# Attention and a squared-ReLU layer on one core: paired transposing DMAs, stores and squares moved to ScalarE, a split last store, and a new planned order

## The chip, the cores and the metric

One core of a Trainium2 chip runs the whole program. Its engines work side by side, each through its own list of instructions in order: TensorE (PE, matrix products into PSUM; PEld is its loading of weights), VectorE (DVE), ScalarE (ACT), GpSimd (POOL) and SyncE (SP). SP, ACT and POOL can issue DMA transfers. An engine waits on semaphores that other engines or landed transfers raise. The metric is the device time of one execution in microseconds (us).

## What is computed

```python
def _attn_ref(q, k, v):                    # (8, 8, 576, 64) each
    B, H, S, D = q.shape
    window = 32
    scores = 1.0 / np.sqrt(D) * np.matmul(q, k.transpose(0, 1, 3, 2))
    pos = np.arange(S)
    mask = np.abs(pos[:, None] - pos[None, :]) <= window
    scores = np.where(mask, scores, -1000000000.0)
    scores = scores - np.max(scores, axis=-1, keepdims=True)
    attn = np.exp(scores)
    attn = attn / (np.sum(attn, axis=-1, keepdims=True) + 1e-09)
    return np.matmul(attn, v).astype(np.float32)

def _moe_ref(x, w_in, w_out):              # (4608, 512), (512, 2048), (2048, 512)
    r = np.maximum(x @ w_in, 0.0)
    return ((r * r) @ w_out).astype(np.float32)

x = attn_out.transpose(0, 2, 1, 3).reshape(B * S, H * D)   # between the two
```

Inputs and the output are float32; the kernel computes its products in bfloat16.

## The kernel before

**Tiles.** The 8 batches of 576 tokens are 4608 tokens. Attention runs in 72 steps of 64 tokens (9 a batch, all 8 heads in one step): `scores` (L468) makes the products of queries with 128 keys (`sc`, line L478), ScalarE the exp (L483), VectorE the mask (L490); `av` (L493) makes the product with the values (`avp`, L505), the reciprocal of the sums (L517) and the scaling into `xr` (L519). `xturn` (L524) turns the step's result so that features lie on partitions, into the ring `xt` of 32 steps: for the first NPE = 26 steps by TensorE (`trp`, L537) and a ScalarE copy (L542), for the other 46 by a transposing DMA on SP (L529), one for each step.

The second half works on 9 tiles of 512 tokens. `mm1` (L547) multiplies `xt` with W1 (`w_in`) into one of two PSUM banks `ht` (products at L53 or, in the 128-token units of the first tile, L51). ScalarE takes the relu (L565), VectorE the square into `gt` (L569). There are 16 such units a tile, numbered k = 0 to 143 over the kernel. `mm2` (L573) multiplies `gt` with W2 (`w_out`) into `outp`, in four segments for each block of 128 tokens; after the fourth, ScalarE copies the block to SBUF (`oe`, L587) and SP stores it (L589). There are 36 blocks. `tile` (L592) records one tile's `mm1` units with the `mm2` segments of the tile before between them.

**Loads.** GpSimd issues all loads from HBM, since they convert to bfloat16. `FIRST` (L37) lists the first 39 in order: pieces of 128 tokens of q, k and v of batches 0 and 1 (the last piece of q and k is 64 tokens, `"e"` are the two ends of v), W1 in the chunks of `WCH` (`"a"`, L423) and W2 in quarters (`"b"`, L430). Batches 0 and 1 of q and k are turned by TensorE (`fine_turn`, L354: products at L364, then a VectorE copy for k, L373, and two ScalarE copies for q, L378). For batches 2 to 7, q and k are loaded raw (`load_qk`, L388), turned in 32x32 blocks by VectorE (`turn`, L438, eight instructions for each of q and k), and moved to their places by small transfers inside SBUF on SP (`spread`, L452, 16 a batch, from `kst` and `qst` to `kt` and `qz`). `copy_v` (L415) makes a copy of v that is shifted by half a tile.

**Order.** Nothing is ordered by hand. Each operation is recorded by `Prog.rec` with an engine, what it reads and writes, a key and an expected duration `dur`; a DMA has also `move` (packets, ns of each). `Prog.schedule` (L103) then runs a list scheduler when the program is built: at each engine, of the operations that its own times hold ready, the one with the lowest key goes next. The list for each engine is fixed by this, and on the chip an engine waits at an operation whose inputs are late although others behind it could run. A transfer is booked as landed 1700 ns after its last packet (`it[3].end = now + 1700` in `serve`, L139); the rings of POOL, SP and ACT take turns. In idle time of TensorE early in the program the planner sets products on a tile of zeros (`zz`), written to `outp`.

The constants at the top set the keys: `LEAD` of the attention steps, `FK`, `FQ` of the first turns, `TOFF`, `TOFF2`, `TST` and `TREL` (a gate) of the VectorE turns, `KQ` and `KVL` of the loads, `VK0`, `VK1`, `VK` of the copies of v, `KM`, `MD`, `TM` of the two products. `UNITS` (L32) is the order of the 16 units of the first tile: (first token, tokens, first of the 16 feature blocks), where feature blocks 4i to 4i + 3 read the i-th quarter of W1.

## Time and profile before

| | |
|---|---|
| median of 3 runs | 317.48 us (316.34, 317.48, 318.16) |
| the profiled execution | 320.36 us |
| its span, first to last instruction | 318.7 us |
| PE busy, products | 303.1 us in 4065 |
| PEld | 205.5 us |
| VectorE | 211.0 us |
| ScalarE | 165.1 us |
| GpSimd | 89.0 us |
| mean granted TensorE clock | 0.988 |
| DMA moved | 38.52 MB in 99291 packets |
| packets of POOL's queue, of SP's | 73136, 26112 |

How to read it: busy times are unions of an engine's instructions and say nothing of whether the work was wanted. Products are pipelined and their ends are modelled, so consecutive products overlap in the rows. The chain of waits goes back from the last instruction, at each step to what released it. In rows of a timeline the first number is the start in us from the span's start, the second the length, and a bracket gives the idle time before and what ended it; a q behind an engine's name is its list of DMA issues. Rows of DMA issues give the count, KB of each and the median us from issue to landing.

### The profile page before, as it was taken

To read this page: it belongs to the slowest core of one execution; us is meant where nothing else is said; L and a number is where in the kernel's file an instruction comes from. 1 tells how busy PE (TensorE), PEld (TensorE's weight loads), DVE (VectorE), ACT (ScalarE), POOL (GpSimd) and SP (SyncE) were. 2 spreads that over 40 slices of the span, in tenths; PEclk is the share of its full clock that TensorE was granted. 3 is DMA by queue.
4 is the path that set the end of the run, shared out by engine and by line. 5 is a ranking of instruction groups with operands and counts; after the bars stand their busy time and mean duration, and the time that the engine had idled before them with its cause. 6 is when DMAs were issued, how large, how long until landed. Compare 5 with 4: busy or idle time off the path is not lost.

```text
span 318.7 us, 9690 instructions
## 1 busy us (share of the span) xinstructions
PE 303.1 (95%) x4065; PEld 205.5 (64%) x4065; DVE 211.0 (66%) x529; ACT 165.1 (52%) x303; POOL 89.0 (28%) x128
## 2 busy tenths in 40 slices
PE   6798999998999999979989999999999999999995
PEld 2466887877977776757546666665665666556552
DVE  7475686958798888868848888898744444323300
ACT  2387767545835662446435645643654555435511
POOL 8999992432142324401504211100000000000000
PEclk9799999999999999999979999999999999999999
DMA  9999999999969948993999596635411211210021
GB/s 58 145 186 200 174 189 187 201 229 237 117 105 183 172 49 129 190 215 48 137 176 161 54 161 102 138 79 110 118 50 51 68 43 43 59 69 33 2 100 67
DMA packets 99291, 38.52 MB, mean 121 GB/s; under 512 B 72624, under 2 KB 93616, under 8 KB 99248
## 3 DMA queue, kind: packets, MB, share of 16 engines
q0 software_dynamic: 73136, 18.36, 60.2%
q1 hardware_dynamic: 26112, 19.54, 22.0%
q8 instruction: 32, 0.52, 0.7%
q14 instruction: 11, 0.09, 0.1%
HBM read 36.70 MB, written 9.44 MB: 145 GB/s over the span
## 4 chain that ended last, share of the span: by engine, by line
PE 77%; DMA 12%; POOL 4%; SPq 2%; DVE 2%; ACT 1%; issue 1%; ACTq 0%
PE outp L53 34%; PE ht L53 33%; DMA qz<-qst 5%; PE sc L478 4%; DMA w<-in_moe_w_in_dram 4%; DMA xt<-xr 3%; PE avp L505 2%; PE ht L51 2%; SPq L452 2%; POOL qfr L351 2%; POOL kfr L351 1%; POOL vd L397 1%; ACT rt L565 1%; PE sc L364 1%; PE trp L537 1%
## 5 line engine op out<-in xcount | busy, mean ns | idle before, releaser
L53 PE MATMUL outp<-w,gt 128*64 128x512 bf16 x1152 | 140.6, 379 | 0.0
L53 PE MATMUL ht<-xt,w 128*64 128x512 bf16 (+1 forms) x1280 | 134.6, 351 | 2.8 <-DMA xt<-xr 2.1
L565 ACT ACTIVATE rt<-ht 128x512 bf16<-128x512 f32 x144 | 85.9, 597 | 70.1 <-PE ht L53 57.7
L53 PEld LDWEIGHTS ht<-xt,w 128*64 128x64 bf16 x1280 | 85.0, 137 | 33.6 <-DMA xt<-xr 3.2
L569 DVE TENSOR_TENSOR gt<-rt 128x512 bf16<-128x512 bf16 x144 | 60.5, 422 | 54.3 <-ACT rt L565 52.8
L53 PEld LDWEIGHTS outp<-w,gt 128*64 128x64 bf16 x1152 | 67.4, 110 | 38.7
L483 ACT ACTIVATE e<-sc 128x512 bf16<-128x512 f32 x72 | 42.2, 595 | 20.1 <-PE sc L478 18.6
L397 POOL DMA_DIRECT2D vd<-in_v_dram x32 | 30.1, 972 | 56.0 <-PE avp L505 26.8
L587 ACT ACTIVATE oe<-outp 128x512 f32<-128x512 f32 x36 | 21.5, 598 | 44.2 <-PE outp L53 44.2
L438 DVE STREAM_TRANSPOSE kst<-kraw 128x256 bf16<-128x256 bf16 (+1 forms) x48 | 37.4, 821 | 0.3 <-DMA kraw<-in_k_dram 0.3
L438 DVE STREAM_TRANSPOSE qst<-qraw 128x256 bf16<-128x256 bf16 (+1 forms) x48 | 36.0, 824 | 0.0
L490 DVE TENSOR_TENSOR pt<-e,mask 128x512 bf16<-128x512 bf16 x72 | 29.8, 417 | 6.4 <-ACT e L483 5.4
L519 DVE TENSOR_TENSOR xr<-avp,rs 128x256 bf16<-128x256 f32 x72 | 30.5, 423 | 1.0
L478 PE MATMUL sc<-qz,kt 128*64 128x128 bf16 x576 | 27.0, 221 | 3.7 <-DMA qz<-qst 3.6
L478 PEld LDWEIGHTS sc<-qz,kt 128*64 128x64 bf16 x576 | 22.2, 111 | 12.1 <-issue 4.6
L517 DVE RECIPROCAL rs<-avp 128x4 f32<-128x4 f32 x72 | 13.1, 181 | 20.2 <-PE avp L505 19.6
L388 POOL DMA_DIRECT2D qraw<-in_q_dram x24 | 15.0, 668 | 23.4 <-DVE qst L438 15.8
L405 POOL DMA_DIRECT2D vx<-in_v_dram x16 | 10.2, 639 | 32.2 <-PE avp L505 27.6
L415 DVE COPY vx<-vd 64x528 bf16<-64x528 bf16 (+1 forms) x28 | 16.9, 608 | 3.1 <-DMA vd<-in_v_dram 2.6
L388 POOL DMA_DIRECT2D kraw<-in_k_dram x24 | 14.7, 653 | 7.9 <-DVE kst L438 7.1
L378 ACT ACTIVATE qz<-sc,half 128x512 bf16<-128x512 bf16 (+1 forms) x20 | 12.1, 647 | 9.1 <-PE sc L364 9.0
L505 PEld LDWEIGHTS avp<-vx,pt 128*64 128x64 bf16 x320 | 11.8, 112 | 4.8 <-issue 0.7
(40 smaller groups left out, 144.6 us busy)
## 6 DMA issues: line engine op xcount, KB each, us to landing
out_dram<-oe SPq DMA_DIRECT2D x36, 256.0 KB, 2.4
vd<-in_v_dram POOLq DMA_DIRECT2D x32, 128.0 KB, 5.7
kraw<-in_k_dram POOLq DMA_DIRECT2D x24, 144.0 KB, 11.2
qraw<-in_q_dram POOLq DMA_DIRECT2D x24, 144.0 KB, 10.0
kt<-kst SPq DMA_DIRECT2D x48, 72.0 KB, 3.4
qz<-qst SPq DMA_DIRECT2D x48, 72.0 KB, 3.5
w<-in_moe_w_out_dram POOLq DMA_DIRECT2D x4, 512.0 KB, 17.4
qfr<-in_q_dram POOLq DMA_DIRECT2D x8, 128.0 KB, 4.9
```

Source lines behind the costliest of these rows:

```text
L53: mm = e.matmul(out[r:r + 64], w[:, r:r + 64], x, start=start, stop=stop)
L388: self.p.rec("POOL", lambda e, g=g, s=s: e.dma_start(raw[32 * g:32 * g + 32], s), writes=[("raw", t, b % 2, g)], dma=(f"{t}{b % 2}", b), k ...
L397: self.p.rec("POOL", lambda e, s=s: e.dma_start(self.VD[i][:, s, :, 0:64], v[b, :, 32 + 128 * s:160 + 128 * s, :].rearrange("h p d -> p h ...
L438: self.p.rec("DVE", lambda e: e.transpose(dst, src), reads=[("raw", t, i, g) for g in range(4)], writes=[("st", t, dh, m0)], key=key, dur= ...
L478: mm = e.matmul(sc[64 * u:64 * u + 64, 128 * j:128 * j + 128], self.KT[i][:, j, at:at + 64], self.QZ[i][:, j, :, 64 * c:64 * c + 64], star ...
L483: self.p.rec("ACT", lambda e: e.activation(self.E[n % 2][:], sc[:], ACTF.Exp, scale=0.125), reads=[("sc", n % 2)], writes=[("e", n % 2)], ...
L490: self.p.rec("DVE", lambda e: e.tensor_tensor(pt, ee, mb, ALU.mult), reads=[("e", n % 2), ("mask", mi)], writes=[("pt", n % 2)], key=key, ...
L505: mm = e.matmul(self.AVP[64 * u:64 * u + 64, VE * j:VE * j + VE], pt[:, 128 * j + 64 * u:128 * j + 64 * u + 64], vt[:, h, 0:VE], start=Tru ...
L519: self.p.rec("DVE", lambda e: e.tensor_tensor(bass.AP(xr, 0, [[256, 128], [64, 4], [1, 64]]), bass.AP(self.AVP, 0, [[512, 128], [VE, 4], [ ...
L565: self.p.rec("ACT", lambda e: e.activation(rt[:], ht[:], ACTF.Relu), reads=[("ht", k % 2)], writes=[("rt", k % 4)], key=key, dur=560)
L569: self.p.rec("DVE", lambda e: e.tensor_tensor(gt[:, d0:d0 + nd, t0:t0 + n], rr, rr, ALU.mult), reads=[("rt", k % 4)], writes=[("gt", T % 2 ...
L587: self.p.rec("ACT", lambda e: e.activation(oe[:], op[:], ACTF.Copy), reads=[("outp", x % 2)], writes=[("oe", x % 3)], old=[("mtmp", 0), (" ...
```

## The change

- `xturn`: the steps from NPE = 27 on go two at a time. `xr` becomes 3 buffers of two steps (it was 4 of one), and at each odd step one transposing DMA on SP turns both.
- `mm2`: the store of a block is issued on ScalarE, behind its copy, and no more on SP.
- `mm1`: for k from 16 to 143 every even unit's square runs on ScalarE as an activation, the odd ones stay on VectorE.
- the last block of 128 tokens is computed in two halves of 256 columns (`mm2_last`), each with its own copy on ScalarE and its own store on SP.
- `fine_turn`: batch 1's copies of k go to ScalarE; `copy_v` may choose an engine (VectorE in all cases).
- W1's second half is loaded as two quarters.
- the planner: a transfer on SP or ACT is booked as landed 3200 ns after its last packet while POOL's ring has a load to serve, 800 ns otherwise; POOL's own keep 1700. Durations of several operations are changed, and the keys of loads, turns, spreads, copies of v and attention steps have a value for each batch. `UNITS` and `FIRST` have another order.

```diff
-NPE = 26
+NPE = 27
 RX = 32
+NXR = 3
 SWITCH = 95
-TOFF, TST, TREL = 5, 0.4, 35
-TOFF2 = 20
-FK, FQ = 14.5, 16.0
-VK0, VK1, VK = 22.0, 1.0, -4.0
-KM, MD, TM = -22.0, 0.5, 3.5
-KQ, KVL = 44, 44
+HWCALM, HWLOAD = 800, 3200
+LB = (5.75, 0.0, -0.25, -3.0, -0.75, 3.75, 2.25, 1.0)
+TB = (22.5, -1.0, -5.0, -4.5, 15.5, 29.5)
+GB = (86.0, 56.0, 67.0, 42.0, 58.0, 11.0)
+TST, SK = 0.7, -27.0
+QB = (70.0, 34.0, 26.0, -78.0, 102.0, 86.0)
+WB = (3.0, 26.0, 54.0, 80.0, 89.0, 54.0)
+VB = (30.5, -13.5, 14.0, -32.5, 0.5, 0.5)
+SQ = (16, 144, 2)
+VENG = ('DVE', 'DVE', 'DVE')
+KENG = ('DVE', 'ACT')
+FK, FQ = 29.75, 18.0
+VK0, VK1 = 9.25, 8.0
+KM, MD, TM = -55.0, 8.0, 3.0
...
 FIRST = (
-    ("v", 0, 2), ("e", 0, False), ("q", 0, 2), ("k", 0, 1), ("q", 0, 0), ("k", 0, 0), ("q", 0, 1),
-    ("k", 0, 2), ("v", 0, 3), ("v", 0, 1), ("v", 0, 0), ("q", 0, 3), ("k", 0, 3), ("q", 1, 0), ("q", 0, 4),
-    ("a", 0, 1), ("k", 0, 4), ("a", 0, 2), ("a", 0, 0), ("k", 1, 0), ("q", 1, 1), ("b", 0, 0), ("v", 1, 3),
...
+    ("v", 0, 1), ("k", 0, 0), ("q", 0, 0), ("k", 0, 2), ("q", 0, 1), ("k", 0, 1), ("v", 0, 2), ("q", 0, 2),
+    ("q", 0, 3), ("v", 0, 0), ("q", 1, 1), ("e", 0, False), ("a", 0, 2), ("k", 1, 2), ("v", 0, 3),
+    ("k", 0, 3), ("a", 0, 1), ("q", 0, 4), ("v", 1, 3), ("k", 0, 4), ("a", 0, 0), ("a", 0, 3), ("k", 1, 0),
...
-WCH = ((0, 512), (512, 512), (1024, 1024))
+WCH = ((0, 512), (512, 512), (1024, 512), (1536, 512))
...
-                    it[3].end = now + 1700
+                    busy = rings["POOL"] and rings["POOL"][0][0] <= now
+                    it[3].end = now + (1700 if q == "POOL" else HWLOAD if busy else HWCALM)
...
     def spread(self, b, t, dh, key):
...
-                           writes=[(t, i, s, r)], old=old, dma=(f"{t}t{i}", b), key=key, dur=600, move=(4, 45))
+                           writes=[(t, i, s, r)], old=old, dma=(f"{t}t{i}{dh}", b), key=key, dur=655, move=(4, 45))
...
     def xturn(self, n):
...
         if n >= NPE:
-            self.p.rec("SP", lambda e: e.dma_start(
-                self.XT[:, n % RX].rearrange("p (j h) q -> p j (h q)", j=2), xr[:], transpose=True),
-                reads=[("xr", n % 4)], writes=[("xt", n % RX)], dma=(f"x{n % 4}", n), key=key, dur=1170, move=(16, 20))
+            if n % 2:
+                self.p.rec("SP", lambda e: e.dma_start(
+                    self.XT[:, (n - 1) % RX:(n - 1) % RX + 2].rearrange("p s (j h) q -> p (s j) (h q)", j=2), xr[:], transpose=True),
+                    reads=[("xr", n // 2 % NXR, 0), ("xr", n // 2 % NXR, 1)], writes=[("xt", (n - 1) % RX), ("xt", n % RX)],
+                    dma=(f"x{n // 2 % NXR}", n), key=key, dur=1400, move=(32, 20))
             return
...
     def mm1(self, T, t0, n, d0, key, mode="col"):
...
-        self.p.rec("DVE", lambda e: e.tensor_tensor(gt[:, d0:d0 + nd, t0:t0 + n], rr, rr, ALU.mult),
+        on = "ACT" if SQ[0] <= k < SQ[1] and k % SQ[2] == 0 else "DVE"
+        dst = gt[:, d0:d0 + nd, t0:t0 + n]
+        self.p.rec(on, lambda e: e.tensor_tensor(dst, rr, rr, ALU.mult) if on == "DVE" else e.activation(dst, rr, ACTF.Square),
                    reads=[("rt", k % 4)], writes=[("gt", T % 2, d0 + d, u) for d in range(nd) for u in us], key=key,
-                   dur=430)
+                   dur=430 if on == "DVE" else 600)
...
     def mm2(self, T, u, seg, key):
...
-        if seg == 3:
+        if seg == 3 and x < NTOK // 128 - 1:
...
-            self.p.rec("SP", lambda e: e.dma_start(self.out[128 * x:128 * x + 128, :], oe[:]),
-                       reads=[("oe", x % 3)], writes=[("out", x)], dma=(f"o{x % 3}", x), key=key, dur=600, move=(8, 80))
+            self.p.rec("ACT", lambda e: e.dma_start(self.out[128 * x:128 * x + 128, :], oe[:]),
+                       reads=[("oe", x % 3)], writes=[("out", x)], dma=(f"o{x % 3}", x), key=key, dur=400, move=(8, 80))
+
+    def mm2_last(self, key):
+        x = NTOK // 128 - 1
+        gt, oe = self.GT[x // 4 % 2], self.OE[x % 3]
+        for h in range(2):
+            op, c = self.OUTP[(x + h) % 2], 256 * h
+
+            def f(e, op=op, c=c):
+                for d in range(16):
+                    mm = matmul(e, "col", op[:, 0:256], gt[:, d, 384:512], self.W2[:, d, c:c + 256], d == 0, d == 15)
+                return mm
...
+            self.p.rec("ACT", lambda e, op=op, c=c: e.activation(oe[:, c:c + 256], op[:, 0:256], ACTF.Copy),
+                       reads=[("outp", (x + h) % 2)], writes=[("oe", x % 3, h)], old=[("oe", x % 3)], key=key + h, dur=390)
+            self.p.rec("SP", lambda e, c=c: e.dma_start(self.out[128 * x:128 * x + 128, c:c + 256], oe[:, c:c + 256]),
+                       reads=[("oe", x % 3, h)], writes=[("out", x, h)], dma=(f"o{x % 3}", x + h), key=key + h, dur=600,
+                       move=(8, 50))
...
     def build(self):
...
-                kb = 9 * b - KQ
+                kb = 9 * b - QB[b - 2]
...
-                kv = 9 * b - KVL
+                kv = 9 * b - WB[b - 2]
...
-                    self.turn(b, t, dh, (0, 3, 5, 7)[m], (3, 2, 2, 2)[m], 9 * b - LEAD - (TOFF if b > 2 else TOFF2) + st // 2 * TST,
-                              9 * b - LEAD - TREL + st // 2 if b > 2 else None)
+                    self.turn(b, t, dh, (0, 3, 5, 7)[m], (3, 2, 2, 2)[m], 9 * b - LEAD - TB[b - 2] + st // 2 * TST,
+                              9 * b - LEAD - GB[b - 2] + st // 2 if GB[b - 2] < 90 else None)
                     if st % 4 == 3:
-                        self.spread(b, t, dh, 9 * b - LEAD - 9)
+                        self.spread(b, t, dh, 9 * b - LEAD - SK)
```

More of the change, by code (lines that the diff above doesn't have):

```diff
@@ L287, in alloc @@
         self.RS = [sb(f"rs{i}", [128, 4], F32) for i in range(2)]
-        self.XR = [sb(f"xr{i}", [128, 256], BF16) for i in range(4)]
+        self.XR = [sb(f"xr{i}", [128, 512], BF16) for i in range(NXR)]
         self.XT = sb("xt", [128, RX, 4, 64], BF16)
@@ L424, in load_w1 @@
                    writes=[("w1", x) for x in range(c // 512, (c + n) // 512)], dma=(f"w1{d}", 0), key=key, dur=770,
-                   move=(32, 88) if n == 512 else (32, 150))
+                   move=(32, 90) if n == 512 else (32, 180))
     def load_w2(self, d, key):
@@ L471, in scores @@
         sc = self.SC[n % 2]
-        key = n - LEAD
+        key = n - LEAD + LB[b]
         def f(e):
@@ L584, in mm2 @@
             self.p.idle_end = self.p.ops[-1]
-        if seg == 3:
+        if seg == 3 and x < NTOK // 128 - 1:
             oe = self.OE[x % 3]
             self.p.rec("ACT", lambda e: e.activation(oe[:], op[:], ACTF.Copy), reads=[("outp", x % 2)],
-                       writes=[("oe", x % 3)], old=[("mtmp", 0), ("mtmp", 1)] if x == 0 else [], key=key, dur=560)
-            self.p.rec("SP", lambda e: e.dma_start(self.out[128 * x:128 * x + 128, :], oe[:]),
-                       reads=[("oe", x % 3)], writes=[("out", x)], dma=(f"o{x % 3}", x), key=key, dur=600, move=(8, 80))
+                       writes=[("oe", x % 3)], old=[("mtmp", 0), ("mtmp", 1)] if x == 0 else [], key=key, dur=600)
+            self.p.rec("ACT", lambda e: e.dma_start(self.out[128 * x:128 * x + 128, :], oe[:]),
[9 more added lines that the diff above has]
+                return mm
+            self.p.rec("PE", f, reads=[("gt", x // 4 % 2, d, 3) for d in range(16)] + [("w2", q) for q in range(4)],
+                       writes=[("outp", (x + h) % 2)], key=key + h, dur=1728, mode="col")
+            self.p.rec("ACT", lambda e, op=op, c=c: e.activation(oe[:, c:c + 256], op[:, 0:256], ACTF.Copy),
[3 more added lines that the diff above has]
+                       move=(8, 50))
     def tile(self, T):
```

50 lines of the change are left out of this document (28 added, 22 removed), and 6 rows, old and new, of the table FIRST.

## The prediction

> **What bounds the kernel now.** I read the page first: engines, then the chain of waits.
>
> ```profile
> span 318.7 us, 9690 instructions
> PE 303.1 (95%) x4065; PEld 205.5 (64%) x4065; DVE 211.0 (66%) x529; ACT 165.1 (52%) x303; POOL 89.0 (28%) x128
> ...
> PE 77%; DMA 12%; POOL 4%; SPq 2%; DVE 2%; ACT 1%; issue 1%; ACTq 0%
> ```
>
> TensorE is busy 303.1 of 318.7 us, and where the chain leaves it, it goes mostly to transfers. But 95% mixes real products with filler products on zeros, so I cut the span into stages: first all PE work, then that on the zero tile alone (start:end, length, busy time, count, granted clock, DMA share, GB/s).
>
> ```profile
> 0.00:30.00 30.00, 23.98 (x369) 0.94 1.51 144
> 30.00:60.00 30.00, 29.60 (x577) 1.00 1.75 187
> 60.00:130.00 70.00, 68.61 (x1004) 1.00 1.07 155
> 130.00:170.00 40.00, 35.59 (x428) 0.96 0.96 152
> 170.00:310.00 140.00, 139.86 (x1654) 1.00 0.37 78
> 310.00:318.70 8.70, 5.49 (x52) 0.96 0.23 90
> ```
>
> ```profile
> 0.00:30.00 30.00, 16.03 (x85) 0.94 1.51 144
> 30.00:60.00 30.00, 0.90 (x8) 1.00 1.75 187
> ```
>
> Time without a useful product, by stage: 0 to 30 us: 30 - 23.98 + 16.03 = 22.0; 30 to 60: 0.4 + 0.9 = 1.3; 60 to 130: 1.4; 130 to 170: 4.4; 170 to 310: 0.1; the end: 3.2. Together 32.4 us. The change leaves the products as they are, so all it can gain is in these six numbers. From 170 us on nothing is left but the end. The stalls in the middle, from TensorE's timeline (the bracket is the idle time and what ended it):
>
> ```profile
> 77.74 0.64 PE L478 MATMUL sc<-qz,kt 128*64 128x128 bf16 x16 [1.07 <-DMA qz<-qst]
> ...
> 141.81 0.41 PE L478 MATMUL sc<-qz,kt 128*64 128x128 bf16 x8 [2.32 <-DMA qz<-qst]
> 142.03 1.92 PE L53 MATMUL ht<-xt,w 128*64 128x512 bf16 x16
> ...
> 160.72 3.37 PE L53 MATMUL ht<-xt,w 128*64 128x512 bf16 x16 [2.10 <-DMA xt<-xr]
> ```
>
> Three waits, 5.5 us, all for transfers from SBUF to SBUF issued on SP. After the last one the same 16 products take 3.37 us instead of 1.92: the stage's clock is 0.96, and this costs 1.45 us more. So 6.9 us stand here.
>
> The Trainium skill, "TensorE: Matmul & The Clock Gate", Part 1, says that the clock halves after an idle window of about 3.4 us. By that rule no wait here would halve it, and 1.45 us less could be won back; the trace has the slow products after 2.10 us, so the trace decides.
>
> **The order and the landings.** The order on each engine is fixed when the program is built. The old planner books a landing 1.70 us after a transfer's last packet, the new one 3.20 us while GpSimd has loads in its ring and 0.80 us otherwise. What the trace has for the same transfers (median us from issue to landing), under loads in the first four rows, late and quiet in the last two:
>
> ```profile
> qz<-qst SPq DMA_DIRECT2D x8, 72.0 KB, 6.0
> qraw<-in_q_dram POOLq DMA_DIRECT2D x4, 144.0 KB, 14.0
> ...
> qz<-qst SPq DMA_DIRECT2D x3, 72.0 KB, 5.3
> ...
> xt<-xr SPq DMA_TRANSPOSE x2, 5.6
> ...
> qz<-qst SPq DMA_DIRECT2D x8, 72.0 KB, 2.1
> ...
> xt<-xr SPq DMA_TRANSPOSE x1, 2.3
> ```
>
> The first is from 64.5 to 71 us, the next from 134.6 to 137.6, then 153.5 to 156, the quiet ones from 222 to 228. The code's own sum for a spread of q or k was 0.60 + 0.60 + 4 x 0.045 + 1.70 = 3.1 us: 1 too long when quiet, 2.9 and 2.2 too short under load. It becomes 0.655 + 0.60 + 0.18 + 3.20 = 4.6 under load and 2.2 quiet: right when quiet, 1.4 and 0.7 short under load. For the transposing transfer it was 1.17 + 0.60 + 0.32 + 1.70 = 3.8 against 5.6, and becomes 5.8. So the error falls by 1.5 us or more in each of the three places. TensorE has other work to put ahead: batches 0 and 1 alone feed two whole tiles of both products. I take the waits as 1.07 to 0, 2.32 to 0.8 and 2.10 to 0.3, the last without the slow products: 5.8 won. The new order has weak places of its own that I can't see; I take off 0.8 and book **5.0** (0 if stalls only move, 6.9 at most).
>
> **The start.** W1 (w_in) now comes in four loads, the 3rd, 2nd, 1st, 4th quarter as items 13, 17, 21, 22 of the list; before it was the 2nd quarter (16), the second half (18), the 1st quarter (19).
>
> ```profile
> 11.25 0.96 POOL L351 DMA_DIRECT2D qfr<-in_q_dram  x1
> 12.12 0.97 POOL L351 DMA_DIRECT2D kfr<-in_k_dram  x1
> ...
> 14.53 0.87 POOL L423 DMA_DIRECT2D w<-in_moe_w_in_dram  x1
> ...
> 15.98 1.63 POOL L423 DMA_DIRECT2D w<-in_moe_w_in_dram  x2
> ```
>
> ```profile
> w<-in_moe_w_in_dram POOLq DMA_DIRECT2D x1, 512.0 KB, 7.6
> ...
> w<-in_moe_w_in_dram POOLq DMA_DIRECT2D x1, 1024.0 KB, 12.4
> ...
> w<-in_moe_w_in_dram POOLq DMA_DIRECT2D x1, 512.0 KB, 14.2
> ```
>
> ```profile
> 28.43 1.08 PE L51 MATMUL ht<-xt,w 128*128 128x128 bf16 x16 [1.00 <-DMA w<-in_moe_w_in_dram]
> ```
>
> Landings before: 14.53 + 7.6 = 22.1, 15.98 + 12.4 = 28.4, and 16.8 + 14.2 = 31.0 (the second of the pair, issued about 0.8 later). These three land one behind the other, so a quarter costs 31.0 - 28.4 = 2.6 us of the queue, half of W1 with a 64 KB piece 6.3. A 128 KB piece costs about 0.87, the issue distance of the first two rows. Counting what stands ahead in the new list: the 2nd quarter has one piece and one quarter more and a 64 KB piece (0.4) less ahead: 22.1 + 0.9 + 2.6 - 0.4 = 25.2. The 3rd has two pieces, a 64 KB one less: 22.1 - 1.7 - 0.4 = 20.0. The 1st has two pieces more, and a quarter in place of the half: 31.0 + 1.7 - (5.9 - 2.6) = 29.4. The 4th: 29.4 + 2.6 = 32.0. The first product with W1 (it needs the 2nd quarter) starts 3.1 us later by this, but two more units of about 0.95 us (16 products, the row of 28.43) can follow it directly, where now TensorE fills with zeros until 28.4; the 1st quarter's unit comes 1.6 earlier, the 4th quarter's 3.6 later. Two units and part of the third: **1.5** won. Ends: -3.1 (the late first landing) to +3.6 (no unit ever waits for the 4th quarter). From 30 to 60 us I book **0.5** of the 1.3, as the same error of landings lies there.
>
> **Squares, stores, transposes.**
>
> ```profile
> L565 ACT ACTIVATE rt<-ht 128x512 bf16<-128x512 f32 x144 | 85.9, 597 | 70.1 <-PE ht L53 57.7 <-PE ht L51 2.9 <-DVE qst L438 2.5
> ...
> L569 DVE TENSOR_TENSOR gt<-rt 128x512 bf16<-128x512 bf16 x144 | 60.5, 422 | 54.3 <-ACT rt L565 52.8
> ...
> L344 ACT ACT_TABLE_LOAD x1 | 1.3, 1283 | 0.7 <-PEq L683 0.7
> ```
>
> 64 squares (even k from 16 to 142) leave VectorE: 64 x 0.422 = 27 us less there. On ScalarE I price one as the relu of the same shape, 0.597 (ends 0.42 to 0.69, by VectorE's and ScalarE's rows): 38 us more. 35 stores leave SP.
>
> ```profile
> 61.28 0.58 SPq L589 DMA_DIRECT2D out_dram<-oe  x1
> ...
> 67.80 0.59 SPq L589 DMA_DIRECT2D out_dram<-oe  x1
> 68.43 2.53 SPq L452 DMA_DIRECT2D qz<-qst  x4
> ```
>
> Here two stores stood among the spreads that end the wait of 77.74, 0.6 us each; their leaving is inside the 1.07 above. On ScalarE 35 x 0.59 = 21 us are added (ends 0 to 35 x 0.6: queue issues in the profile are not counted as busy), and each waits for its own copy first and holds the relus and exps behind it, whose reader is TensorE's next product into the same bank. The five 0.42 us copies of batch 1's k become about 0.69 on ScalarE. ScalarE then has 165 + 38 + 21 + 3 = 227 of 310 us, 73%; VectorE 211 - 27 - 2 = 182. Hidden, so **0**, as long as ScalarE keeps room; in its fuller stretches:
>
> ```profile
> 100.00:110.00 10.00, 6.27 (x12) 1.00 1.07 189
> ```
>
> Eight of those twelve are relus: four squares (2.4) and a store (0.6) make 9.3 of 10. There the cover is thin.
>
> 46 transposing transfers become 23 (27, 29, ... 71); one was 1.25 us of SP. A double one is unknown: 1.25 to 2.5 us, so SP saves 0 to 29 us; I take 1.4, nearer to one issue than two. A step now waits for its partner before it is sent, and SP holds the spreads queued behind that wait, which TensorE's scores of the next batch read; xt's ring holds four tiles, so the later step hurts nobody at once, and the order is planned with the wait: **0**, down to the 2.10 of another wait on xt where it fails. Step 26 goes on TensorE: 0.1 us there, and is sent again with step 27, unread in between.
>
> **The end.**
>
> ```profile
> 315.60 0.60 ACT L587 ACTIVATE oe<-outp 128x512 f32<-128x512 f32 x1 [2.92 <-PE outp L53]
> ```
>
> From the copy's start the span has 3.1 us. The last copy is half as wide: about 0.4 instead of 0.6, and half of the bytes follow. I take **0.4** (0.1 to 0.8).
>
> **Sum.** 5.0 + 1.5 + 0.5 + 0.4 = 7.4. The profiled execution took 320.36 us (1.7 around its span), so 313.0 by its own time; it ran 2.9 above the median of 317.48, from which the forecast is **310.0**.
>
> **Rivals.**
> 1. *Nearly all waits go and the start gains its full bound.* 6.9 + 3.6 + 1.0 + 0.5 = 12: 305.5. For it: the work to fill with is there. Against: under load the bookings stay short. 0.17.
> 2. *The stalls only move.* The new order keeps about 5 of the 6.9 elsewhere, since one constant can't follow landings from 2.1 to 6.0 us; start even. 317.5 - 1.9 - 0.4 = 315.2; in its worse half nothing is left. 0.15.
> 3. *ScalarE becomes the bound.* Squares and stores stand ahead of relus, the two banks of ht stay full, TensorE waits on relu. If 20 of 64 squares put their 0.6 us ahead of a relu for which TensorE waits: 12.0 - 7.4 = 4.6 slower, 322. It decides from 13 squares on (13 x 0.6 = 7.8). For it: 9.3 of 10 in the full stretch; against: 73% overall, and the old idle time before relus, 57.7 us for PE. 0.16.
> 4. *Square forces table loads.* The trace has one load, 1.283 us, with exp, relu and copy in use; a square is new. If each change between square and exp needed one, some 100 loads make 128 us: 227 + 128 = 355 on ScalarE alone, about 360. 0.02.
>
> The Trainium skill, "ScalarE: Activation LUTs", What ACT_TABLE_LOAD costs, has the same 1283 ns and adds about 1380 of drain, which would make it 130 us worse still; its list of fillers in every set names relu and copy but not square. No run here shows a square.
>
> **Chances.** The forecast 0.50, the rivals 0.17, 0.15, 0.16, 0.02. Within 0.5% (315.9 to 319.1) this measurement can't tell a change from none. Faster: 0.50 + 0.17 + 0.08 of rival 2 = 0.75; same 0.07; slower 0.16 + 0.02 = 0.18. The likeliest case alone spans 306 to 314 (its terms at 3.5 to 11). The range for 8 in 10 is 303.5 to 319.5: outside lie most of rivals 3 and 4 (0.15) and the low tail of rival 1 (0.05).
>
> **What would show it.** The waits of qz, kt and xt on TensorE between 60 and 170 us under 2 us and its clock 1.00 there; W1's first product near 25 us, filler under 16 us; ScalarE near 205 us busy with one table load; relu rows with TensorE, not ScalarE, as what they wait for; 23 transposes on SP; under 3 us after the last product. I am wrong if TensorE's idle time before products is ended by relu or square, if the middle's idle time stays over 5 us, or if the first 60 us lose more than 23.3.

## The result, and the profile after

| | before | after |
|---|---|---|
| median of 4 runs each, in turn on one chip | 317.62 us (316.34 to 318.16) | 312.62 us (312.17 to 313.40) |
| the profiled execution | 320.36 us | 312.32 us |
| its span | 318.7 us | 310.5 us |
| mean granted TensorE clock | 0.988 | 1.00 |

The ratio is 0.9851, with a 95% interval of 0.9814 to 0.9888: 5.0 us faster. The forecast was 310.0 (303.5 to 319.5).

From the page of the kernel after: engines, then the chain of waits, and the group of the moved squares.

```profile
span 310.5 us, 9706 instructions
PE 301.4 (97%) x4117; PEld 222.4 (72%) x4117; DVE 184.4 (59%) x460; ACT 200.9 (65%) x374; POOL 89.1 (29%) x129
...
PE 82%; DMA 7%; DVE 5%; POOL 4%; SPq 1%; issue 1%; ACT 0%; POOLq 0%; DVEq 0%
...
L586 ACT ACTIVATE gt<-rt 128x512 bf16<-128x512 bf16 x64 | 40.4, 631 | 1.5 <-PE outp L62 0.3
```

VectorE lost 26.6 us of work and ScalarE gained 35.8, 35 stores are now issued on ScalarE, and ScalarE has no share of the chain (0%): what the chain lost is DMA, from 12% to 7%. TensorE's stages (start:end, length, busy time, count, granted clock, DMA share, GB/s), and under them the zero tile alone:

```profile
0.00:30.00 30.00, 24.15 (x377) 1.00 1.60 145
30.00:60.00 30.00, 30.00 (x574) 1.00 1.60 193
60.00:130.00 70.00, 69.74 (x1052) 1.00 1.36 176
130.00:170.00 40.00, 39.47 (x480) 1.00 1.03 158
170.00:300.00 130.00, 129.96 (x1548) 1.00 0.31 69
300.00:310.50 10.50, 8.04 (x107) 1.00 0.20 76
```

```profile
0.00:30.00 30.00, 15.90 (x97) 1.00 1.60 145
30.00:60.00 30.00, 1.03 (x8) 1.00 1.60 193
```

Time without a useful product, worked out as it was for before, with the 1.45 us of half-speed products counted in the middle:

| stage | before | after | gain | predicted |
|---|---|---|---|---|
| 0 to 30 us | 22.0 | 30 - 24.15 + 15.90 = 21.75 | 0.3 | 1.5 |
| 30 to 60 us | 1.3 | 1.03 | 0.3 | 0.5 |
| 60 to 170 us | 1.4 + 4.4 + 1.45 = 7.25 | 0.26 + 0.53 = 0.79 | 6.5 | 5.0 |
| the end | 3.2 | 10.5 - 8.04 = 2.5 | 0.7 | 0.4 |
| sum | | | 7.8 | 7.4 |

The spans differ by 8.2 us. The gain lies where it was looked for, in the middle. Nearly all that is left there are these two stalls on TensorE's timeline (start, length, and in the bracket the idle time before and what ended it):

```profile
76.08 0.64 PE L491 MATMUL sc<-qz,kt 128*64 128x128 bf16 x16 [0.26 <-DMA qz<-qst]
...
155.02 1.95 PE L62 MATMUL ht<-xt,w 128*64 128x512 bf16 x16 [0.44 <-issue]
```

The profile names no releaser for the second. It too is a wait for a transfer: a transposing DMA into `xt`, issued at 149.84, landed 5.1 us later, at 154.9, just ahead of these products. So the waits on q, k and xt are 0.70 us here.

How the wait on batch 4's queries (before: 2.32 us at 141.81) went is seen in three engines. First before, then after: the last block transpose on VectorE, the spreads on SP, and the score on TensorE that needs them.

```profile
130.70 0.76 DVE L438 STREAM_TRANSPOSE qst<-qraw 128x256 bf16<-128x256 bf16 x1
...
133.91 3.74 SPq L452 DMA_DIRECT2D qz<-qst  x4
```

```profile
125.41 1.31 DVE L451 STREAM_TRANSPOSE qst<-qraw 128x256 bf16<-128x256 bf16 x2
...
124.81 4.49 SPq L465 DMA_DIRECT2D qz<-qst  x6
...
136.63 0.42 PE L491 MATMUL sc<-qz,kt 128*64 128x128 bf16 x8
```

Before, the last block was turned at 130.70 + 0.76 = 131.5, the last spread issued at 137.7, and it landed 0.1 us ahead of the score's start at 141.8. After, the turn ends at 125.41 + 1.31 = 126.7 and the last issue at 129.3. The landing itself was no faster (6.5 us from issue to landing for the last two, 5.0 before), but it came at 135.9, 0.7 ahead of the score at 136.6. SP needed 6.2 us from the last turn to the last issue before, and 2.6 after. Batch 5 is alike: its q landed at 176.5 before, 0.2 us ahead of its score; after, at 168.3, 1.8 ahead.

So the trace shows *that* VectorE's turns and SP's spreads come earlier. Several parts of the change could be the reason, which is what the experiments had to tell apart: the squares that left VectorE, the stores that left SP, the halved number of transposing DMAs, the bookings of landings, the durations, or the order alone, whatever engine runs what.

### The profile page after: what moved, and what is told of

It reads as the page before. It is cut to its first block, busy times and chain, and to the rows that moved or that the text cites. A ratio compares the mean times of both kernels' runs of the same rounds, so it can differ in the third digit from the quotient of the medians.

```text
span 310.5 us, 9706 instructions
## 1 busy us (share of the span) xinstructions
PE 301.4 (97%) x4117; PEld 222.4 (72%) x4117; DVE 184.4 (59%) x460; ACT 200.9 (65%) x374; POOL 89.1 (29%) x129
## 4 chain that ended last, share of the span: by engine, by line
PE 82%; DMA 7%; DVE 5%; POOL 4%; SPq 1%; issue 1%; ACT 0%; POOLq 0%; DVEq 0%
PE outp L62 37%; PE ht L62 33%; PE sc L491 5%; PE avp L518 3%; PE ht L60 3%; DMA vd<-in_v_dram 3%; DMA qz<-qst 2%; DVE kst L451 2%; DVE qst L451 2%; DMA kt<-kst 2%; POOL qfr L361 1%; SPq L465 1%; POOL kfr L361 1%; POOL vd L409 1%; PE trp L552 1%; PE sc L374 1%
## 5 line engine op out<-in xcount | busy, mean ns | idle before, releaser
L62 PE MATMUL outp<-w,gt 128*64 128x512 bf16 (+1 forms) x1184 | 140.4, 373 | 0.0
L62 PE MATMUL ht<-xt,w 128*64 128x512 bf16 (+1 forms) x1280 | 132.3, 348 | 0.5 <-issue 0.4
L62 PEld LDWEIGHTS ht<-xt,w 128*64 128x64 bf16 x1280 | 93.5, 136 | 22.5 <-issue 1.3
L62 PEld LDWEIGHTS outp<-w,gt 128*64 128x64 bf16 x1184 | 74.7, 110 | 32.7
L586 DVE TENSOR_TENSOR gt<-rt 128x512 bf16<-128x512 bf16 x80 | 33.7, 422 | 47.9 <-ACT rt L581 40.4
L409 POOL DMA_DIRECT2D vd<-in_v_dram x32 | 29.2, 922 | 56.4 <-PE avp L518 37.1
L586 ACT ACTIVATE gt<-rt 128x512 bf16<-128x512 bf16 x64 | 40.4, 631 | 1.5 <-PE outp L62 0.3
L451 DVE STREAM_TRANSPOSE kst<-kraw 128x256 bf16<-128x256 bf16 (+1 forms) x48 | 36.7, 828 | 1.8 <-DMA kt<-kst 1.8
```

The source lines that it names most:

```text
L62: mm = e.matmul(out[r:r + 64], w[:, r:r + 64], x, start=start, stop=stop)
L409: self.p.rec("POOL", lambda e, s=s: e.dma_start(self.VD[i][:, s, :, 0:64], v[b, :, 32 + 128 * s:160 + 128 * s, :].rearrange("h p d -> p h ...
L451: self.p.rec("DVE", lambda e: e.transpose(dst, src), reads=[("raw", t, i, g) for g in range(4)], writes=[("st", t, dh, m0)], key=key, dur= ...
L586: self.p.rec(on, lambda e: e.tensor_tensor(dst, rr, rr, ALU.mult) if on == "DVE" else e.activation(dst, rr, ACTF.Square), reads=[("rt", k ...
```

## Experiments

Each ratio is to the kernel before, run in turn on the same chip. A change of an engine or a booking makes the planner choose a new order for everything ("planned anew" below). In a "held" kernel the order of every engine's list is the one that the named kernel has, and only the engine that runs an operation is exchanged, at the planned place. That separates what an engine costs from what the plan does with it.

### The kernel before, profiled again

No edit.

> The kernel before, unchanged, profiled a second time. Its first profile had a span of 318.7 us, though its runs have a median of 317.6, which with 1.7 us around the span is a span near 315.9. If the first profiled execution was an unlucky one: a span near 316, the waits of TensorE on qz and xt between 60 and 170 us well under 5.5 us, and a clock of 1.00 there. If the waits belong to the plan and the 2.9 us lie elsewhere: again about 5.5 us of waits and products at half clock near 160 us.

318.43 us in its one run, span 316.8, clock 0.999. TensorE's timeline:

```profile
76.63 0.64 PE L478 MATMUL sc<-qz,kt 128*64 128x128 bf16 x16 [0.88 <-DMA qz<-qst]
...
129.90 1.95 PE L53 MATMUL ht<-xt,w 128*64 128x512 bf16 x16 [2.47 <-DMA xt<-xr]
...
141.25 0.41 PE L478 MATMUL sc<-qz,kt 128*64 128x128 bf16 x8 [0.46 <-DMA qz<-qst]
...
160.65 1.95 PE L53 MATMUL ht<-xt,w 128*64 128x512 bf16 x16 [2.59 <-DMA xt<-xr]
```

The span and the clock came as expected of a luckier execution, the waits did not: they come to 6.4 us here, 5.5 in the first profile, but not at the same places: one on xt at 129.9 is new, the one on qz at 141 is nearly gone. After both waits of some 2.5 us the products ran at full speed (1.95 us for 16). The order is the same in both executions, so where a late landing shows depends on the execution.

### The new bookings alone, and the kernel after with the old ones

```diff
-                    it[3].end = now + 1700
+                    busy = rings["POOL"] and rings["POOL"][0][0] <= now
+                    it[3].end = now + (1700 if q == "POOL" else 3200 if busy else 800)
```

> The kernel before with the new bookings of landings alone (3.2 us under load, 0.8 quiet), keys and engines unchanged. If the bookings make the order good: TensorE's waits on qz, kt and xt under 2 us and 313 to 315 us. If the moves of work or the new keys do it: the waits stay or move, 316.5 to 319 us.

316.54 us (315.24 to 321.15), ratio 0.9926, interval 0.9879 to 0.9973. TensorE's timeline:

```profile
139.62 0.41 PE L479 MATMUL sc<-qz,kt 128*64 128x128 bf16 x8 [1.89 <-DMA qz<-qst]
...
159.60 1.95 PE L53 MATMUL ht<-xt,w 128*64 128x512 bf16 x16 [3.17 <-DMA xt<-xr]
...
218.68 1.95 PE L53 MATMUL ht<-xt,w 128*64 128x512 bf16 x16 [0.59 <-DMA xt<-xr]
```

The wait near 77 us is gone, the one before 139.6 is 1.89, the one on xt grew from 2.10 to 3.17, and a small one appeared at 218.68: 5.65 us together. The time lies at the lower edge of what was expected if the waits stay or move, and they did: with the old keys the better bookings mostly move the stalls.

The other way round, in the kernel after, planned anew:

```diff
-HWCALM, HWLOAD = 800, 3200
+HWCALM, HWLOAD = 1700, 1700
```

> The changed kernel with every landing booked 1.7 us after the last packet, as before; all else kept. If the bookings make the order good: TensorE waits 3 us or more on qz, kt or xt between 60 and 170 us, 315.5 to 318 us. If the moves of work do it: under 1.5 us of such waits, 312 to 313.5 us.

315.73 us (313.93 to 319.73), ratio 0.9904, interval 0.9868 to 0.9940. TensorE's timeline:

```profile
77.16 0.64 PE L491 MATMUL sc<-qz,kt 128*64 128x128 bf16 x16 [1.08 <-DMA qz<-qst]
...
108.98 0.64 PE L491 MATMUL sc<-qz,kt 128*64 128x128 bf16 x16 [1.49 <-DMA qz<-qst]
...
141.51 0.41 PE L491 MATMUL sc<-qz,kt 128*64 128x128 bf16 x8 [1.84 <-DMA qz<-qst]
```

4.4 us of waits on qz, where after has 0.26. The squares, stores and double transposes are all in this kernel, so without the new bookings they do not take the waits away in this plan. The keys are still those chosen beside the new bookings; what keys chosen for the old ones would reach was not tried.

### The squares

First the kernel after with all squares on VectorE, planned anew:

```diff
-SQ = (16, 144, 2)
+SQ = (0, 0, 2)
```

> The changed kernel with all squares on VectorE again, planned anew. If VectorE was only off the path: 312 to 313.5 us, VectorE 27 us busier, ScalarE 40 us less. If its relief is what brought the turned q and k in time: waits on qz and kt come back, 314.5 us or more.

328.13 us (326.16 to 329.18), ratio 1.0295, interval 1.0220 to 1.0371: 4.4 points above after's ratio, the largest effect of all. Taken by itself, this run would make the squares' move the whole change and more. Its waits of TensorE (us in total, times, longest) and its VectorE between 130 and 133 us:

```profile
PE avp L518 <- DVE xr L532: 6.4, 8, 1.2
```

```profile
130.26 0.74 DVE L451 STREAM_TRANSPOSE qst<-qraw 128x256 bf16<-128x256 bf16 x1
...
131.19 0.41 DVE L532 TENSOR_TENSOR xr<-avp,rs 128x256 bf16<-128x256 f32 x1
131.51 1.01 DVE L451 STREAM_TRANSPOSE kst<-kraw 128x384 bf16<-128x384 bf16 x1
```

The attention steps run here in a row, each with its reciprocal, mask and scaling and then a block transpose, and TensorE waits about 1 us for each scaled step (`xr`). No square stands between 125 and 136 us. VectorE is full (10.70 of those 11 us), but with turns and attention. After such waits the products themselves ran at half speed: from 132 to 136 us, with a granted clock of 0.50, and again near 206 us, where 16 products take 3.59 us instead of 1.92:

```profile
206.37 3.59 PE L62 MATMUL ht<-xt,w 128*64 128x512 bf16 x16
```

So the run does not show that a square on VectorE is dear; it shows that the plan with them is another one. To tell the two apart, the same engine for the squares with after's order held:

```diff
+            op.eng, op.plan = op.plan, op.eng
...
+        for op in ops:
+            op.eng = op.plan
...
-        self.p.rec(on, lambda e: e.tensor_tensor(dst, rr, rr, ALU.mult) if on == "DVE" else e.activation(dst, rr, ACTF.Square),
+        self.p.rec("DVE", lambda e: e.tensor_tensor(dst, rr, rr, ALU.mult),
...
-                   dur=430 if on == "DVE" else 600)
+                   dur=430 if on == "DVE" else 600, plan=on)
```

> The changed kernel's own order on every engine, with the 64 squares run on VectorE at the place in time that the plan gave them on ScalarE; nothing planned anew. If VectorE's load itself makes the turned q and k late: the last q of batches 4 and 5 lands 3 us or more later than in the changed kernel (135.9, 168.3), TensorE waits on xr and qz, ratio to the kernel before 1.0 or more. If it was only the new plan that made all squares on VectorE so slow (ratio 1.03): 0.985 to 0.993 here.

312.96 us (311.43 to 314.08), ratio 0.9802, interval 0.9758 to 0.9846. All 144 squares are on VectorE:

```profile
L589 DVE TENSOR_TENSOR gt<-rt 128x512 bf16<-128x512 bf16 x144 | 60.0, 424 | 44.6 <-ACT rt L584 35.3 <-PE outp L62 7.1 <-PE ht L62 1.6
```

The interval overlaps that of after, so this kernel can't be called faster than it. At this order it makes no difference that these runs can measure on which of the two engines the squares run, and batch 4's q lands at 135.6 (after 135.9).

The kernel before with the 64 squares on ScalarE, planned anew with its own keys and bookings:

```diff
-        self.p.rec("DVE", lambda e: e.tensor_tensor(gt[:, d0:d0 + nd, t0:t0 + n], rr, rr, ALU.mult),
+        on = "ACT" if 16 <= k < 144 and k % 2 == 0 else "DVE"
+        dst = gt[:, d0:d0 + nd, t0:t0 + n]
+        self.p.rec(on, lambda e: e.tensor_tensor(dst, rr, rr, ALU.mult) if on == "DVE" else e.activation(dst, rr, ACTF.Square),
...
-                   dur=430)
+                   dur=430 if on == "DVE" else 600)
```

> The kernel before with the 64 squares on ScalarE and nothing else, planned anew with its own keys and bookings. If VectorE's load alone made q and k late: the last q of batches 3 to 5 lands 2 us or more earlier than 109.1, 141.7 and 176.5, ratio 0.985 to 0.992. If the squares help only together with the earlier turns that the new keys ask for: the waits stay, ratio 0.995 to 1.005.

315.48 us (313.95 to 317.90), ratio 0.9868, interval 0.9815 to 0.9921: this edit alone, planned anew, comes to 1.3% of after's 1.5%, and its interval holds after's 0.9851. Batch 4's q lands at 134.1 and batch 5's at 156.4 (before 141.7 and 176.5), which is what was expected if VectorE's load alone made them late. The same edit with before's order held tells whether it did:

```diff
+        on = "ACT" if 16 <= k < 144 and k % 2 == 0 else "DVE"
...
-                   dur=430)
+                   dur=430, plan="DVE")
```

> The kernel before with its own order on every engine, and the 64 squares run on ScalarE at the time planned for VectorE. If only the order counts: waits and landings as before (the last q of batch 4 near 141, of batch 5 near 175), ratio 0.996 to 1.004. If VectorE's room counts by itself: batches 3 to 5 land 2 us earlier or more, ratio 0.99 or less.

320.82 us (318.68 to 322.10), ratio 1.0060, interval 1.0027 to 1.0092: nothing of the gain is left. The last q of batches 4 and 5 lands at 141.2 and 176.0, as in before. The stalls on TensorE's timeline are of before's kind again:

```profile
109.38 0.64 PE L481 MATMUL sc<-qz,kt 128*64 128x128 bf16 x16 [1.27 <-DMA qz<-qst]
...
141.38 0.41 PE L481 MATMUL sc<-qz,kt 128*64 128x128 bf16 x8 [1.57 <-DMA qz<-qst]
...
161.01 3.36 PE L53 MATMUL ht<-xt,w 128*64 128x512 bf16 x16 [2.71 <-DMA xt<-xr]
```

The four together:

| | squares on VectorE | 64 of them on ScalarE |
|---|---|---|
| before's order | 1 | 1.0060 (1.0027 to 1.0092) |
| after's order | 0.9802 (0.9758 to 0.9846) | 0.9851 (0.9814 to 0.9888) |

The rows differ by some 2%, the columns by no more than 0.6%, and not in ScalarE's favour. So the engine of the squares does not make the gain at either order. The rows differ in the order, and in the other edits of the change too: the stores and the double transposes, which come next, the loads of W1, batch 1's copies of k, and the split last block, whose end is worth 0.7 us in the table of stages. The squares' move matters in the plan, where VectorE counts as freer: planned anew, the last q block of batch 4 is turned by 124.4 us, against 131.5 in before and 130.6 with before's order held, although VectorE was rid of the same 64 squares there.

### The stores, and the double transposing DMA

The kernel after with its order held, the 35 stores issued on SP:

```diff
-            self.p.rec("ACT", lambda e: e.dma_start(self.out[128 * x:128 * x + 128, :], oe[:]),
+            self.p.rec("SP", lambda e: e.dma_start(self.out[128 * x:128 * x + 128, :], oe[:]),
...
-                       reads=[("oe", x % 3)], writes=[("out", x)], dma=(f"o{x % 3}", x), key=key, dur=400, move=(8, 80))
+                       reads=[("oe", x % 3)], writes=[("out", x)], dma=(f"o{x % 3}", x), key=key, dur=400, move=(8, 80), plan="ACT")
```

> The changed kernel's own order, with the 35 stores issued on SP at the planned time in place of ScalarE. If SP's issue time was worth something: 0.6 us for each store ahead of a spread, landings of q and k in batches 2 to 5 up to 1.5 us later, ratio 0.988 to 0.995. If not: 0.983 to 0.988, as the changed kernel.

313.73 us (312.89 to 314.05), ratio 0.9825, interval 0.9792 to 0.9859. Batch 4's q lands at 137.3 and batch 5's at 171.4, 1.4 and 3.0 later than in after. TensorE's timeline at the first scores of batches 2, 4 and 5:

```profile
76.43 0.64 PE L494 MATMUL sc<-qz,kt 128*64 128x128 bf16 x16 [0.77 <-DMA qz<-qst]
...
137.44 0.41 PE L494 MATMUL sc<-qz,kt 128*64 128x128 bf16 x8 [0.55 <-issue]
...
171.46 0.64 PE L494 MATMUL sc<-qz,kt 128*64 128x128 bf16 x16 [0.66 <-issue]
```

The last two have no releaser named, but each starts 0.1 us behind the landing of its q, so all three are waits for q: 2.0 us, where after has 0.26. So the stores do take SP's time ahead of the spreads, and TensorE waits for it. In the times it does not show: the later landings came as expected, the higher ratio did not.

The kernel after with one transposing DMA for each step (45 of them, for steps 27 to 71), planned anew:

```diff
-            if n % 2:
-                self.p.rec("SP", lambda e: e.dma_start(
-                    self.XT[:, (n - 1) % RX:(n - 1) % RX + 2].rearrange("p s (j h) q -> p (s j) (h q)", j=2), xr[:], transpose=True),
+            self.p.rec("SP", lambda e: e.dma_start(
+                self.XT[:, n % RX].rearrange("p (j h) q -> p j (h q)", j=2), xr[:, o:o + 256], transpose=True),
-                    reads=[("xr", n // 2 % NXR, 0), ("xr", n // 2 % NXR, 1)], writes=[("xt", (n - 1) % RX), ("xt", n % RX)],
-                    dma=(f"x{n // 2 % NXR}", n), key=key, dur=1400, move=(32, 20))
+                reads=[("xr", n // 2 % NXR, n % 2)], writes=[("xt", n % RX)], dma=(f"x{n % 6}", n), key=key, dur=1250, move=(16, 20))
```

> The changed kernel with one transposing transfer for each step again (46, from the same three double buffers), planned anew. One transfer for two steps took 1.20 us of SP in the changed kernel, so 23 x 1.2 = 28 us come back on SP. If SP's room matters: spreads late, waits on qz or kt, ratio 0.99 to 1.0. If not: 0.983 to 0.988.

315.39 us (314.40 to 318.27), ratio 0.9886, interval 0.9849 to 0.9922. The tile xt's rows (min/median/max ns, first and last start) in after, and in this kernel:

```profile
L543 SPq DMA_TRANSPOSE xt<-xr x23: 1189/1199/1578, 110.9 to 258.7; - x23
```

```profile
L542 SPq DMA_TRANSPOSE xt<-xr x45: 1167/1195/2175, 113.2 to 264.7; - x45
```

A double transfer takes no longer to issue than a single one, so pairing saves SP 45 x 1.195 - 23 x 1.199 = 26.2 us. The profile has 1.7 us of waits on qz and 1.4 on xt, and the ratio falls between the two that were expected. As this was planned anew, it can't be told whether SP's time or the other plan made the waits; the interval overlaps after's.

### The bookings and the measured durations, with the old keys

```diff
+                    it[3].end = now + (1700 if q == "POOL" else 3200 if busy else 800)
...
-                        dur=190 + 140 * n)
+                        dur=330 + 100 * n)
...
-                    dur=40 + 320 * n, gate=gate)
+                    dur=170 + 290 * n, gate=gate)
...
-                           writes=[(t, i, s, r)], old=old, dma=(f"{t}t{i}", b), key=key, dur=600, move=(4, 45))
+                           writes=[(t, i, s, r)], old=old, dma=(f"{t}t{i}", b), key=key, dur=655, move=(4, 45))
```

These are the landings, the copies of v, VectorE's turns and the spreads; beside them go relu, exp and the copy of a block from 560 to 600, the transposing DMA from 1170 to 1250, the copy of the last piece of k in batches 0 and 1 from 300 to 430, and the packets of W1's quarters and of its half from 88 and 150 ns to 90 and 180.

> The kernel before with the new bookings of landings and the measured durations (relu, exp, copies 600, VectorE turns 170 + 290 each, spreads 655, copies of v, one transposing transfer 1250, W1's packets), keys and engines as before. If a true clock in the planner is enough: waits on qz, kt and xt under 1.5 us, ratio 0.98 to 0.99. If it needs keys that give it an order to choose: the waits go, but idle time or late turns take their place, ratio 0.99 to 1.0.

321.02 us (319.13 to 323.44), ratio 1.0056, interval 1.0018 to 1.0094: slightly slower than before. TensorE's timeline:

```profile
130.71 0.32 PE L506 MATMUL avp<-vd,pt 128*64 128x65 bf16 x8 [1.57 <-DVE pt L491]
...
132.42 6.56 PE L53 MATMUL ht<-xt,w 128*64 128x512 bf16 x32 [1.39 <-DMA xt<-xr]
```

The waits on the spreads of k and q are gone from TensorE; what comes instead is a wait on a masked tile, three on xt (2.1 us in all), and a run of 32 products that takes 6.56 us where full speed makes it about 3.8. A planner with truer times does not by itself make a better order. That the old keys had been chosen to suit the old times is a likely reason, which no run tests.

### The start: W1's second quarter first

The kernel after with the loads of W1's 2nd and 3rd quarters exchanged in `FIRST`, and the units that read them in `UNITS`:

```diff
-    (0, 128, 0), (128, 128, 4), (128, 128, 12), (128, 128, 8), (256, 256, 2), (0, 128, 4), (256, 256, 6),
+    (0, 128, 0), (128, 128, 4), (128, 128, 12), (0, 128, 4), (256, 256, 2), (128, 128, 8), (256, 256, 6),
...
-    ("q", 0, 3), ("v", 0, 0), ("q", 1, 1), ("e", 0, False), ("a", 0, 2), ("k", 1, 2), ("v", 0, 3),
-    ("k", 0, 3), ("a", 0, 1), ("q", 0, 4), ("v", 1, 3), ("k", 0, 4), ("a", 0, 0), ("a", 0, 3), ("k", 1, 0),
+    ("q", 0, 3), ("v", 0, 0), ("q", 1, 1), ("e", 0, False), ("a", 0, 1), ("k", 1, 2), ("v", 0, 3),
+    ("k", 0, 3), ("a", 0, 2), ("q", 0, 4), ("v", 1, 3), ("k", 0, 4), ("a", 0, 0), ("a", 0, 3), ("k", 1, 0),
```

> The changed kernel with W1's second quarter loaded 13th and the third 17th, and in the list of units the two that read them exchanged, planned anew. If W1's quarters set the start: W1's first product near 23 us in place of 25.7, filler in 0 to 30 us down by 1.5 us or more, the end 1 to 2 us earlier. If the steps of attention set it: the first product may come earlier, filler falls by under 0.7 us, ratio 0.980 to 0.990.

313.73 us (312.57 to 316.12), ratio 0.9824, interval 0.9778 to 0.9870. In after the 2nd quarter is issued at 14.97 and lands 9.6 later, at 24.6; here it is issued at 11.67 and lands 7.5 later, at 19.2. TensorE's timeline:

```profile
23.98 0.30 PE L552 MATMUL trp<-ident,xr 128*64 128x128 bf16 x4 [0.44 <-DVE xr L532]
...
25.31 1.90 PE L60 MATMUL ht<-xt,w 128*128 128x128 bf16 x16
```

5.4 us earlier on the chip brought the first product with W1 from 25.71 to 25.31, 0.4 earlier, and no gain that can be measured (313.49 us for after on this chip). The product's unit is (128, 128, 4), which reads steps 2 and 3. Step 3's turn (`trp`) stands at 23.98 here, and ScalarE's copy of it into `xt` ends at 24.7, 5.5 us behind W1's landing. In after step 3 is turned at 23.45 and copied by 24.2, W1's quarter lands at 24.6, and the product starts at 25.71, behind the turn of step 4 and 6 filler products that the list puts ahead of it. So W1's landing alone does not set this start, as the second of the expectations has it. This profile can't price it: its products ran at half speed here (16 in 1.90 us, 1.08 in after), and it is of the longest of the kernel's four runs.

### The kernel after, once more

No edit, on the chip of `b_held_squares_act`, `b_all_times` and the exchanged quarters.

> The changed kernel again, beside the other three on one chip: ratio 0.980 to 0.989, TensorE's waits on qz, kt and xt between 60 and 170 us under 1 us.

313.49 us (312.30 to 315.30), ratio 0.9833, interval 0.9784 to 0.9882. Span 310.5 again, so two profiles of each kernel stand beside one another. TensorE's stages from 60 us, first of before (second profile), then of after (second profile):

```profile
60.00:130.00 70.00, 66.47 (x977) 1.00 1.12 159
130.00:170.00 40.00, 36.95 (x460) 1.00 0.99 152
```

```profile
60.00:130.00 70.00, 69.12 (x1034) 1.00 1.33 175
130.00:170.00 40.00, 38.71 (x474) 1.00 1.05 155
```

3.53 + 3.05 = 6.6 us idle before, 0.88 + 1.29 = 2.2 after: the middle gains 4.4 here (the two profiles are of different chips), 6.5 in the first pair. The 2.2 us left in after are again waits for transfers from SBUF to SBUF: 0.26 on qz, and 0.62 and 1.29 ahead of products at 125.56 and 155.23, each of which starts within 0.1 us of the landing of a transposing DMA. That is more than the 1 us expected.

## Why the prediction came out as it did

**The place of the gain: right.** "Three waits, 5.5 us, all for transfers from SBUF to SBUF issued on SP" are the time that went. The middle won 6.5 us in the first pair of profiles and 4.4 in the second; 5.0 was booked. Clock 1.00 there and waits of qz, kt and xt under 2 us were named as the sign; the first profile has 0.70, the second 2.2, just over it.

**The reason given for it: half wrong.** The error of the bookings "falls by 1.5 us or more in each of the three places"; the step from there to shorter waits failed for the bookings by themselves. Put alone into before, they made it 0.7% faster with 5.65 us of waits left; with the measured durations beside them it was slower than before. Undone in after, with the keys kept, they bring some 4 us of waits back. So they are not sufficient, and with these keys they are needed: they work together with the keys and the engines that the planner counts with. How much each of the keys does was not tried. That 5.0 came out so near is in part luck, as it was priced for the bookings alone. Rival 2, stalls that only move, is what the bookings did in before's plan; it did not come true in after.

**Squares on ScalarE at 0: right at a held order, wrong in the plan.** One takes 631 ns (597 priced), ScalarE is busy 200.9 us (near 205 forecast), there is one table load as before, and ScalarE's idle time before the relu is still ended by TensorE:

```profile
L581 ACT ACTIVATE rt<-ht 128x512 bf16<-128x512 f32 x144 | 85.3, 595 | 40.6 <-PE ht L62 35.4 <-PE ht L60 2.6 <-DVE gt L586 0.5
...
L354 ACT ACT_TABLE_LOAD x1 | 1.3, 1283 | 0.7 <-PEq L722 0.7
```

Rivals 3 (ScalarE as the bound) and 4 (table loads) fall with these rows. (The 130 us that rival 4 adds come to 138 by its own figures, which changes nothing.) What the step did not see is that the planner plans with the squares: on before's keys their move, planned anew, is worth 1.3%, and at the same order held it is worth nothing.

**The stores: right at 0 as far as the times can tell.** The held run shows no difference, though its trace has 1.7 us more of waits for q; their price on ScalarE's queue was too high (35 x 0.59 against 0.34 each). **The double transposes: right at 0 as far as seen**, the price of one too high (1.4 against 1.20).

**The start: the step that failed.** 1.5 was booked for 0 to 30 us, and 0.3 and 1.0 came (1.0 in the second pair: 21.4 less 20.4). The landings of W1 were forecast well (2nd quarter 25.2, measured 24.6; 3rd 20.0 and 19.5; 1st 29.4 and 28.8; 4th 32.0 and 31.3), and so was the first product "near 25". What failed is "two more units of about 0.95 us can follow it directly". TensorE's units in after, and ScalarE's relus between them:

```profile
25.71 1.08 PE L60 MATMUL ht<-xt,w 128*128 128x128 bf16 x16
...
27.58 1.07 PE L60 MATMUL ht<-xt,w 128*128 128x128 bf16 x16
...
29.34 1.98 PE L60 MATMUL ht<-xt,w 128*128 128x128 bf16 x32
```

```profile
26.84 0.60 ACT L581 ACTIVATE rt<-ht 128x512 bf16<-128x512 f32 x1 [1.24 <-PE ht L60]
...
28.68 0.60 ACT L581 ACTIVATE rt<-ht 128x512 bf16<-128x512 f32 x1 [0.24 <-PE ht L60]
```

The second unit starts 1.87 us after the first and the third 1.76 after the second, each within 0.15 us of the end of the relu before it. The kernel has the reason: unit k writes bank k % 2 of `ht`, and in each bank the units keep the order of `UNITS`. The even bank begins with (0, 128, 0), which needs the 1st quarter of W1 (landed at 28.8). The three units that can run before it are k = 1, 3 and 5, all in the odd bank, so each must wait until ScalarE has taken the one before. The same distance stands between the last two of them in the run with the quarters exchanged (28.04 and 29.81). A list of units that alternates the banks here was not tried. The run with the quarters exchanged shows besides that the 2nd quarter's landing does not set the first unit's start by itself. And the first unit came not 3.1 us later than in before but 1.9 (25.71 against 23.82), and 0.1 in the second pair: before's had not started with the landing of its quarter at 22.2, as the working took it. From 30 to 60 us, 0.5 was booked and 0.3 and -0.25 came.

**The end: right, a little small.** 0.4 was booked, 0.7 came in both pairs. The last copy on ScalarE's timeline in after:

```profile
308.08 0.38 ACT L622 ACTIVATE oe<-outp 128x256 f32<-128x256 f32 x1 [1.30 <-PE outp L62]
```

From the last copy's start the span has 310.5 - 308.08 = 2.4 us, where it had 3.1.

**The number: 2.6 us too low, the measured time well inside the range.** The sum of 7.4 fits the pair of profiled executions that it was made for (spans 8.2 apart), but it was taken at full size off a median that lies 2.9 below that execution. In the second pair the terms are 1.0 - 0.25 + 4.4 + 0.7 = 5.9, with no half-speed products in before, and its spans differ by 6.3; the medians fell by 5.0 and, on the chip of the second profile of after, by 6.1 (319.58 to 313.49). So the step that mis-sized the number is the last of the sum, in which the losses of one long execution, the 1.45 us of half-speed products among them, were booked as losses of a median one; beside it stands the start's term, which was 0.5 to 1.2 too large.

## What to carry to other kernels

When an order is planned by a program, an edit to the cost or engine of one operation can change the order of all; to learn what the operation itself is worth, hold the order and exchange it there. Here an effect of 4.4 points (squares back on VectorE, planned anew) turned into none that could be measured. And before the gain of a wait is taken off a median, profile the kernel twice: stalls that come and go between executions can be worth less than one trace shows.

## What the runs showed of the hardware

- A transposing DMA of 128x512 occupies SP's queue for 1.199 us by the median, one of 128x256 for 1.195 in the same kernel with single transfers: between these two sizes the issue does not grow. The prediction had 1.25 to 2.5 for the larger.
- A store's issue takes about the same on both queues, and longer beside other issues: 0.338 us by the median on ScalarE in after, 0.352 on SP in the held kernel, and 0.58 to 0.60 on SP where spreads stood next to it. The row of ScalarE's stores in after (min/median/max ns):

```profile
L606 ACTq DMA_DIRECT2D out_dram<-oe x35: 338/338/374, 54.0 to 305.3; - x35
```

- A square of 128x512 from SBUF in bfloat16 takes ScalarE 631 ns, more than the relu of the same shape from PSUM in float32 (595); VectorE takes 422.
- Products ran at about half speed after waits of 2.10 and 2.71 us and after one of 1.39 that followed one of 1.57 closely, and at full speed after waits of 2.32, 2.47, 2.59 and 3.17 us. With all squares on VectorE, planned anew, they ran at half speed after rows of waits of which none was longer than 1.2 us. The length of the last wait alone does not decide it.

The Trainium skill, "TensorE: Matmul & The Clock Gate", Part 1, has the clock halve after an idle window of about 3.4 us that runs freely, without regard to when the kernel started. That the outcome varies between executions of one order, as in the two profiles of before, agrees with a free-running window; that waits of 2.10 and 2.71 us were enough, and rows of shorter ones, does not agree with the length that it gives. What decides was not measured here.
